# Row scalings and adds in place of diagonal matrix products in a gated S5 + linear-attention kernel

## The chip, the cores and the metric

The kernel runs on one core of one Trainium2 chip. The metric is the device time of one execution in microseconds. Before the change it is 169.73 us, the median of 3 runs (169.57 to 170.41). All work is in bf16 with f32 accumulation; TensorE (PE) multiplies matrices into PSUM, VectorE (DVE), ScalarE (ACT) and GpSimd (POOL) work on 128-partition tiles, and SyncE (SP) issues most DMAs.

## The reference, cut to what matters

The output is `g * a + (1 - g) * b` for 2048 positions of 512 channels, from one input x. The gate g is the sigmoid of one dot product per position.

```python
# a: a diagonal complex state-space layer (512 states)
Lam_bar = exp(dt * Lam);  B_bar = ((Lam_bar - 1) / Lam)[:, None] * Bmat
for t in range(L):  h = Lam_bar * h + B_bar @ x[t]
a = 2 * Re(hseq @ Cmat.T) + x * Dskip
# b: linear attention, 32 heads of 16 channels
phi = concat(softmax(p), softmax(-p))      # of q @ w_phi and of k @ w_phi
b = (phi_q @ (phi_k.T @ v)) / (phi_q @ sum(phi_k)) @ wo
```

## The kernel before, in words

**State-space half.** The 2048 positions are split by residue r = position mod 4, so the scan runs over 512 steps of four positions. x is loaded transposed as `xT`, 16 tiles of 128 positions ordered by residue. For a block j of 128 states (four blocks), `g{j}{dst}{ri}` (`st_g`, L541) multiplies x by B and by the decayed B, LBT = Lam_bar B, for the real or imaginary part ri: `g..0.` is the first phase of two positions (residues 0, 1), `g..1.` the second (residues 2, 3), to which the first, decayed by Lam_bar squared, is added by two products with diagonal matrices (L555, L556). `z{j}` (`st_z`, L581) turns the complex scan into two real scans by rotating with cosine and sine tables (T2c, T2s, made by `i{j}`), and writes the states H3. `h{j}{ri}` (`st_h`, L613) gives the states after the first phase, H1 = M * H3(previous) + U1, by two diagonal products into PSUM (L621, L622) and one DVE add out of PSUM (L625). `c` (`st_c`, L561) makes C2 = C times B's factor by two diagonal products (L575, L576) and a copy out by ACT; `r` and `b` (`st_r` L653, `st_b` L661) make C3 = Lam_bar C2 by one ACT scaling into f32 and one DVE multiply-add. `p` (`st_p`, L531) makes LBT from the loaded B by diagonal products of 256 columns (L535, L536) and an ACT copy. The diagonal matrices `dg` are nine per state block; `D` (`st_D`, L372) builds them on DVE out of `dgs`, the 128 x 1 factors that `M` (`st_M`) computes on POOL.

**Attention half.** `W`, `f`, `w` fold w_phi into the key and query weights. `k`, `v`, `q` (L427 to L446) project a tile of 128 positions by four 512-column products and copy it out of PSUM (`Xq` holds keys, later queries). A feature group is `x` (tree of maxima, subtract), `n` (tree of minima, subtract), `e` (exp on ACT, one 128x1024 instruction a tile), `s` (tree of sums, log, exp, multiply): `feat_max` L465 to `feat_sum` L485. Key groups have two tiles (8 groups), query groups two for the first four tiles (A, B) and four for the rest (X1 to X3). `a` accumulates phi_k.T v and the gate's dot product.

**Tail.** `END` frees pools. For each of 16 output tiles n, in residue order 3, 1, 0, 2: `y{n}` (L692) accumulates the state-space output in a PSUM bank (8 products with H3 or H1, then 4 with K0T or the diagonal Dd), `o{n}` (L713) multiplies phi_q by the key-value matrix (pn), takes the denominator's reciprocal as exp(-ln) on ACT and scales on DVE (L733) into `on`, which a DMA transposes into oT (L739); `t{n}` (L742) adds oT times Wo to the same bank (L746), scales by the gate into `ot` (ACT, or DVE where the token says `:D`) and stores it.

**What sets the order.** `tc.manual_schedule` keeps PE, DVE, ACT and SP in program order, and the program order is the list ORDER: each token is the next step (up to a `yield`) of the generator of that name; `@` gives the PSUM banks (0 to 7) it takes and `:D` puts the step's copy or scaling on DVE in place of ACT. Every engine runs its own instructions strictly in this order and waits by semaphores for the others. DMA transposes are all issued by SP, in its queue, before or in this order. POOL is not in the manual schedule; it runs in the program's order too. The loads of x, B, C and the weights are issued ahead of the list (L221 to L240).

Of the kernel before, what the change touches and what calls it, by code (L numbers as in the profile page):

```python
# [10 lines left out]
ALU = mybir.AluOpType  # L11
AX = mybir.AxisListType
ACT = mybir.ActivationFunctionType
F32 = mybir.dt.float32
# [10 lines left out]
W0@0 V@1 B B V W3@2 U B W0 W2@3 P P P2 P2 W3 U B P2 P2 W2 P2 W1@4 P P4 P3 P4 U W1 f1@5 f2@6 f0@7 f3@1 P4 U P2 v1@0 P3  # L25
v0@2 i1 i0 i1 i0 f1 f2 f3 v1 f0:D i0 k1@3 i0 i0 i2 i1 k1 i1 k0@4 i2 i3 i1 M i2 k0:D i2 k3@5 v0 k2@6 i3 x0 k4@1 n0 k3
x0 n0 v6@7 i2 v5@0 x0 V2@3 n0 i3 i3 k2 x0 n0 k7@4 x0 x1 i3 D k4 n0 v6 L k5@2 n1 k6@5 x1 n1 p32@6 p10@1 x1 e0 p20@7 k6
n1 p02@5 V2 e0 k5:D v3@3 x1 D p30@2 n1 p20 x1 n1 n2 x2 n2 v4@7 s0 p32 x2 v3 s0 x2 s0 p10 e1 v5 n2 k7 p00@6 gw x2 v2@3
p12@1 s0 p30 p22@0 p00 D s0 v7@4 n2 e1 p02 x2 n2 g000@2 s1 s0 n3 s1 x3 n3 x3 v2 s0 g101@6 s1 k8@5 x3 e2 v4 s1 e2 v7 k8
s2 g101 n3 g000 s2 s1 x3 s1 g000 k9@3 a0@74 g001@5 p12 g101 s2 n3 k9 a0 s1 k11@2 s2 x3 n3 s2 s2 e3 n4 x4 n4 k12@1 k11  # L30
a1 x4 k13@6 n4 x4 n4 x4 g001 a1 k10@3 s2 e3 g010@2 x4 k10 n4 a2 s3 n5 g010 g011@3 x5 n5 s3 x5 s3 x5 a2 s3 p22 e4 x5 n5
e4 g011 s4 x5 w3@0 k13 n5 g001 k12 s3 k14@6 s4 w3 n5 s3 s4 g010 v8@5 x6 s3 k14 g011 w1@1 e5 g010 x6 n6 g011 v9@0 s4 s4
a3 v8 e5 w0@6 g100@2 n6 k15@3 v9 s4 x6 z0 z0 n6 z0 k15 x6 g111@5 s5 w1 n6 z0 a3 s4 x6 s5 n6 w0 w2@0 s5 g100 w2 n7 g111
x7 n7 v13@3 g110@1 g100 g111 e6 g110 q1@6 x7 e6 z0 a4 g110 s5 n7 a4 x7 q0@0 v10@2 g111 s6 z0 g110 x7 g200@5 v11@1 n7
s6 x7 n7 s5 z0 v10 s5 g201@2 v13 g211@3 z1 q0 z0 z1 g201 s6 v11 q1 s5 s6 z1 nA z0 e7 e7 z0 xA q2@0 g210@1 g200 s7 s6
g211 nA a5 xA g201 v12@6 z1 nA xA s7 nA s6 q3@2 a5 z1 g210 xA g200 z1 c00@5 s7 z1 q3 xA q2 c00 z1 v12 nA xB z1 nB
v15@2 c13@0 xB s6 g211 eA g310@5 s7 g300@6 g210 eA sA g310 nB v15 g211 s7 g210 sA z1 xB g311@2 z2 z2 nB g301@3 z2
v14@1 s7 g301 nB g300 s7 g311 xB a6 g301 sA z2 g300 g310 sA g311 z2 sA g310 c13 a6 z2 q7@3 sA sA q10@6 z2 g311 xB q8@5
v14 nB c12@0 z2 sA z3 c10@2 eB eB c10 q13@1 a7 q6@2 z3 q13 h01@1 q8 z2 sB c02@5 a7 z3 z3 sA sB c12 z2 q7 z3 Y h01 Y
c01@0 z3 c02 sB q10 c03@3 c11@5 z3 c11 sA q4@6 h00@1 h20@7 c03 sB h21@5 q6 c01 r0 q12@3 h00 z3 sB sB h11@2 G h20 z3  # L40
q12 z3 sB q9@0 h10@1 h10 sB q5@3 h31@7 h30@1 h11 q9 Y q11@0 r1 sB h31 q4 h30 sB h21 q5 END o0@6 Y o0 X1 N1 q11 o1@3 X1
y1@2 N1 q14@7 X1 G K2@0 N1 o0@1 X1 N1 K2 o0 o1 X1 o0 q15@5 N1 o1@4 o0 o1 y1 o0 r1 o0 K3@0 y0@6 q14 o1 q15 K1@7 E1 o1
E1 E1 E1 X2 N2 o1 o3@5 K1 y3@1 N2 X2 o3 o3@3 y2@4 o2@7 o3 N2 y0 b0 K3 o2 y1 S1 N2 o3 S1 y3 X2 S1 r0 o3 y7@0 X2 S1 X2
S1 y2 o2@5 o2 o3 S1 S1 y0 y6@3 y3 N2 S1 o1 t1 G y6 o2 t0 o2 X3 o2 b1 o3 E2 S1 E2 N3 E2 E2 K0@7 t3 G X3 S1 o4@5 t0 o2
y5@6 t1 K0 t3 S2 S2 b0 o4 r2 y2 b1 o5@2 o5 o5@7 o4@1 y5 S1 t3 S1 o5 o4 S2 o5 t2 o5 o5 y4@2 o4 S2 o5 r3 o6@7 S2 y7 o4
o4 o6 S2 b2 y4 S2 o4 o7@5 t2 S2 o6@1 r2 y5 o6 o6 y7 r3 y4 t5 S2 o7 t5 o7@4 b3 o7 X3 X3 b2 b3 y6 t4 o6 y8@6 o6 o7 N3
y9@7 o7 y8 o8@1 N3 o7 S2 o6 y14@5 t4 o9@2 X3 o9 o9@4 N3 t5 y9 N3 o9 o7 o9 o9 E3 t1 S2 o8 t6 o8@2 E3 o8 y8 t7 y14 t6:D
o9 E3 o10@3 o8 E3 t7 o8 o8 o10 S3 S3 y10@4 t0 o10@1 t4 o10 y9 y11@2 o10 t6 S3 o10 S3 o9 t9 o10 y10 S3 S2 t9 o8 o11@0
# [18 lines left out]
def kernel(  # L67
# [96 lines left out]
    nc.scalar.dma_start(out=Wv[:], in_=B_wqkv[:, 2 * D:3 * D].rearrange("(k p) n -> p k n", p=P))  # L164
# [4 lines left out]
    Wk2 = const.tile([P, KT, D], BF16, name="Wk2")  # L169
# [42 lines left out]
    BrT = pAC.tile([P, KT, Pst], BF16, name="BrT")  # L212
    BiT = pAC.tile([P, KT, Pst], BF16, name="BiT")
    LBT = pAC.tile([P, KT, 2, Pst], BF16, name="LBT")
    LBrT, LBiT = LBT[:, :, 0, :], LBT[:, :, 1, :]
# [17 lines left out]
    for ti in range(8, NTI):
        x_load(ti)
    for j in range(KT):
        nc.sync.dma_start_transpose(out=WTq[:, j, :], in_=B_wqkv[:, j * P:(j + 1) * P])
# [581 lines left out]
```

## Time and profile before

| What | Before |
|---|---|
| Median of 3 runs (all) | 169.73 us (170.41, 169.73, 169.57) |
| Span of the profiled execution, first to last instruction | 168.6 us |
| What lies around the span, against the median | 1.1 us |
| PE busy (share), matmuls | 157.2 us (93%), 1062 |
| DVE busy (share), instructions | 145.0 us (86%), 355 |
| ACT busy (share), instructions | 113.2 us (67%), 234 |
| POOL busy | 6.7 us (4%) |
| First projection (pv) / first pn product / last Wo product ends | 9.39 / 99.56 / 165.10 us |
| DMA packets, bytes | 50710, 15.94 MB |

Busy times are sums over the profiled execution. A matmul's listed duration is longer than the interval at which matmuls follow each other: 4 products of 512 columns show as 379 ns each, and a block of four starts every 0.86 us, 0.216 us each. The same holds, by less, for DVE and ACT: an instruction that starts right behind another overlaps its beginning. Below, the interval from start to start in a back-to-back row is called the step, and it is what sums are made of; the steps are read off the start times in the timeline.

### The profile page before, as it was taken

The numbers are of one execution on the slowest core, as the hardware profiler recorded it, in microseconds if no ns is written. First come the engines' busy times: TensorE is split into PE (matmuls) and PEld (weight loads), VectorE is DVE, ScalarE is ACT, GpSimd is POOL, SyncE is SP. The second block draws the span as 40 slices with busy tenths as digits, with TensorE's granted clock in tenths as the row PEclk, the third lists the DMA queues.
The fourth block names the chain that finished last, engine by engine and source line by source line (L and its number), as shares of the span: only waits on it lengthen the run. The fifth ranks groups of instructions, "written<-read, shape, count | busy, mean of one in ns | idle before, by whom it ended". The sixth has DMA issues, their size and how long they took to land.

```text
span 168.6 us, 2978 instructions
## 1 busy us (share of the span) xinstructions
PE 157.2 (93%) x1062; PEld 80.5 (48%) x1062; DVE 145.0 (86%) x355; ACT 113.2 (67%) x234; POOL 6.7 (4%) x23
## 2 busy tenths in 40 slices
PE   0699999999999999999999999999999959999991
PEld 0554466465555544544544444455456424445440
DVE  3796999999999999999999999999999937843540
ACT  3789999989988667374688853974987158404203
POOL 3072010000000000000000000000000000000000
PEclk9999999999999999999999999999999999999999
DMA  4945984546446300000006023111589564669543
GB/s 128 219 92 138 239 136 102 109 95 88 102 93 97 125 2 0 0 4 0 0 4 124 0 53 71 31 35 31 135 179 97 127 171 131 166 159 124 125 125 124
DMA packets 50710, 15.94 MB, mean 95 GB/s; under 512 B 46088, under 2 KB 50696, under 8 KB 50696
## 3 DMA queue, kind: packets, MB, share of 16 engines
q1 hardware_dynamic: 49112, 14.70, 43.1%
q10 hardware_dynamic: 1584, 1.07, 2.2%
q8 instruction: 8, 0.13, 0.4%
q14 instruction: 6, 0.05, 0.1%
HBM read 2.64 MB, written 2.10 MB: 28 GB/s over the span
## 4 chain that ended last, share of the span: by engine, by line
DVE 67%; PE 21%; issue 4%; DMA 4%; ACT 2%; SPq 0%; DVEq 0%; ACTq 0%
DVE smk L460 8%; DVE w L600 5%; PE py L746 5%; DVE EEk L496 5%; DVE mxk L460 5%; DVE mnk L460 5%; PE py L708 4%; DVE EEk L470 4%; DVE EEk L476 4%; DVE on L733 3%; PE py L701 3%; PE py L702 3%; DVE smq L460 3%; DVE H L625 3%; DMA C2r<-in_B_wqkv_dram 2%
## 5 line engine op out<-in xcount | busy, mean ns | idle before, releaser
L425 PEld LDWEIGHTS <-xT 128*128 128x128 bf16 x192 | 18.5, 100 | 20.4 <-issue 2.3
L733 DVE SCALAR_TENSOR_TENSOR on<-pn,RG,rd 128x256 bf16<-128x256 f32 x32 | 14.3, 475 | 10.1 <-ACT rd L134 8.2
L134 ACT ACTIVATE EEk<-EEk 128x1024 bf16<-128x1024 bf16 x20 | 20.9, 1068 | 3.0 <-DVE EEk L476 2.9
L425 PE MATMUL pv<-Wv,xT 128*128 128x512 bf16 x64 | 17.7, 409 | 0.0
L750 ACT ACTIVATE ot<-py,G 128x512 bf16<-128x512 f32 x11 | 7.5, 687 | 13.6 <-PE py L746 8.3
L425 PE MATMUL pq<-Wq,xT 128*128 128x512 bf16 x64 | 16.1, 378 | 0.1
L746 PE MATMUL py<-Wo,oT 128*128 128x512 bf16 x64 | 16.1, 379 | 0.0
L551 PE MATMUL pgq<-xT,LBT 128*128 128x512 bf16 x64 | 15.6, 379 | 0.0
L425 PE MATMUL pk<-Wk,xT 128*128 128x512 bf16 x64 | 15.3, 379 | 0.0
L115 ACT CAST uv<-pgq 128x512 bf16<-128x512 f32 x16 | 9.3, 585 | 6.6 <-PE pgq L551 4.4
L134 ACT ACTIVATE ld<-pn 128x16 f32<-128x16 f32 x32 | 5.4, 186 | 11.0 <-PE pn L724 10.8
L134 ACT ACTIVATE EEq<-EEq 128x1024 bf16<-128x1024 bf16 x12 | 11.9, 1045 | 0.6 <-DVE EEq L476 0.6
L702 PE MATMUL py<-Wv,H 128*128 128x512 bf16 x32 | 12.1, 379 | 0.0
L702 PE MATMUL py<-C2i,H 128*128 128x512 bf16 x32 | 12.1, 379 | 0.0
L701 PE MATMUL py<-Wk,H 128*128 128x512 bf16 x32 | 12.1, 379 | 0.0
L701 PE MATMUL py<-C2r,H 128*128 128x512 bf16 x32 | 12.1, 378 | 0.0
L115 ACT CAST vx<-pv 128x512 bf16<-128x512 f32 x16 | 9.6, 600 | 1.7 <-PE pv L425 1.7
L724 PEld LDWEIGHTS <-phT 128*128 128x128 bf16 x128 | 7.2, 98 | 7.4 <-issue 2.3
L115 ACT CAST Xq<-pq 128x512 bf16<-128x512 f32 x16 | 9.1, 587 | 2.4 <-PE pq L425 2.4
L724 PE MATMUL pn<-KVm,phT 128*128 128x68 bf16 x128 | 8.1, 194 | 2.0 <-ACT ot L750 2.0
L496 DVE TENSOR_TENSOR EEk<-EEk,rck 128x2048 bf16<-128x2048 bf16 x8 | 9.7, 1214 | 0.0
L460 DVE TENSOR_TENSOR smk<-smk 128x512 bf16<-128x512 bf16 (+2 forms) x30 | 9.7, 322 | 0.0
(168 smaller groups left out, 338.0 us busy)
## 6 DMA issues: line engine op xcount, KB each, us to landing
out_dram<-ot SPq DMA_DIRECT2D x16, 128.0 KB, 2.0
C2r<-in_B_wqkv_dram ACTq DMA_DIRECT2D x1, 512.0 KB, 4.0
Wv<-in_B_wqkv_dram ACTq DMA_DIRECT2D x1, 512.0 KB
Bn_r<-in_A_B_re_dram SPq DMA_DIRECT2D x1, 512.0 KB, 4.8
Bn_i<-in_A_B_im_dram SPq DMA_DIRECT2D x1, 512.0 KB
Wo<-in_B_wo_dram SPq DMA_DIRECT2D x1, 512.0 KB
xT<-in_A_x_dram SPq DMA_TRANSPOSE x16, 3.4
oT<-on SPq DMA_TRANSPOSE x16, 2.3
```

The source lines that it names most:

```text
L115: nc.scalar.copy(out=out_ap, in_=in_ap)
L134: ins = nc.scalar.activation(**kw)
L425: MM(out=pt[:], lhsT=xT[:, kt, ti * P:(ti + 1) * P], rhs=W[:, kt, :], start=(kt == 0), stop=(kt == KT - 1))
L460: VT(out=t[:], in0=cur[:, :, :, 0:n, :], in1=cur[:, :, :, n:2 * n, :], op=op)
L496: VT(out=E5, in0=E5, in1=rc[:].to_broadcast([P, L, 2 * NB, Dh, 4]), op=ALU.mult)
L551: MM(out=pgq[:], lhsT=LBT_[:, kt, js], rhs=xT[:, kt, (r1 - 1) * NC:r1 * NC], start=False, stop=(r1 == 1 and kt == KT - 1))
L600: nc.vector.tensor_tensor_scan(out=w[:, ri, :], data0=rb, data1=ut[:, ri, :], initial=0.0, op0=ALU.mult, op1=ALU.add)
L701: MM(out=py[:], lhsT=src[:, j, 0, off:off + P], rhs=cr[:, j, :], start=(j == 0), stop=False)
L702: MM(out=py[:], lhsT=src[:, j, 1, off:off + P], rhs=ci[:, j, :], start=False, stop=False)
L724: MM(out=pn[:, 4 * m:4 * m + 4, :].rearrange("p h e -> p (h e)"), lhsT=ph[:, 4 * hf + m, :], rhs=KVm[:, 4 * hf + m, :], start=(m == 0), st ...
L733: nc.vector.scalar_tensor_tensor(out=on[:, 2 * hf:2 * hf + 2].rearrange("p g h e -> p (g h) e"), in0=pns[hf][:, :, 0:Dh], scalar=RG[:, ti: ...
L746: MM(out=py[:], lhsT=oT[:, g, :], rhs=Wo[:, g, :], start=False, stop=(g == HG - 1))
```

## The change: what it does

- LBT, C2, C3 and H1 are no longer made by products with diagonal matrices (C3: by an f32 scaling and a multiply-add). Each is now two scalings of a real-imaginary pair (128 x 1024, by a 128 x 1 factor, `scaled`, on ACT unless the token says `:D`) and two 512-wide adds or subtracts on DVE; H1 has a 1024-wide add of U1 besides. LBT is then transposed by a DMA from SBUF (`l`, new `st_l`).
- Only the three diagonal matrices of L555/L556 are still built.
- Key groups are now of 2, 2, 4, 4, 2, 2 tiles and the first query group of 4. Their buffers come from one pool.
- DMA transposes are wider: x in 9 DMAs (two of one tile, seven of two), B in 4 from SBUF, Wq in 2, C in 4; and they are issued as steps of the list (`Lx`, `Ln`, `Lb`, `Lq`, `Lc`, `Lo`). The five small parameter loads go from SP to POOL.
- 12 products of a zero tile (`Z`) are issued on PE at the start.
- The gate's factor in the attention output goes into the bias of the exp (L738 after), so that `on` is a two-operand multiply.
- The list ORDER is written anew; all key copies out of PSUM are on ACT, and seven of the `ot` scalings on DVE (five before).

```diff
 ORDER = """
-W0@0 V@1 B B V W3@2 U B W0 W2@3 P P P2 P2 W3 U B P2 P2 W2 P2 W1@4 P P4 P3 P4 U W1 f1@5 f2@6 f0@7 f3@1 P4 U P2 v1@0 P3
...
+Lx Lx Z@0 Z Lx Z Z Z Z Z Z Z Z Z Z V@1 W0@0 V W0 Lx B W2@2 U B W3@3 W3 P W1@4 W1 P B P2 Lx W2 P2 B P2 V2@5 V2 P2 f0@0
+P gw P2 P4 f3@2 U f1@4 P2 f0 f2@3 P4 f3 f1 f2 P3 P4 i0 i2 k0@1 i0 U i0 i0 i0 k1@3 P3 i2 i2 k3@4 Ln k0 Ln k1 Lx Lx Lq U
...
+KGROUPS = ((0, 2), (2, 2), (4, 4), (8, 4), (12, 2), (14, 2))
+XLOADS = ((0, 1), (1, 1), (2, 2), (4, 2), (6, 2), (8, 2), (10, 2), (12, 2), (14, 2))
...
-            nc.sync.dma_start(out=t_[4 * n:4 * n + 4, :], in_=src.rearrange("(j p) -> j p", p=P))
+            nc.gpsimd.dma_start(out=t_[4 * n:4 * n + 4, :], in_=src.rearrange("(j p) -> j p", p=P))
...
+            trans(out=xT[:, :, t0_ * P:(t0_ + n) * P], in_=x_res[t0_ // 4, c0:c0 + n * P])
...
+            trans(out=BT[:, :, :, j * P:(j + 1) * P].rearrange("p r k s -> p (r k) s"), in_=Bn[:, j].rearrange("p r d -> p (r d)"))
...
+    def st_Z():
+        pz = bank([P, D], F32, "pz")
+        while True:
+            MM(out=pz[:], lhsT=warm[:, 0:P], rhs=warm[:], start=True, stop=True)
+            yield
...
+    def scaled(out_ap, in_ap, s_):
+        if sel["eng"] == "act":
+            nc.scalar.mul(out=out_ap, in_=in_ap, mul=s_)
+        else:
+            VS(out=out_ap, in0=in_ap, scalar1=s_, scalar2=None, op0=ALU.mult)
+
+    def st_l(j):
+        lr, li = uv[j][:, 0], uv[j][:, 1]
+        scaled(lr, Bn[:, j], dgs[:, S_LR, j:j + 1])
+        yield
+        scaled(li, Bn[:, j], dgs[:, S_LI, j:j + 1])
+        yield
+        VT(out=lr[:, 0], in0=lr[:, 0], in1=li[:, 1], op=ALU.subtract)
+        yield
+        VT(out=lr[:, 1], in0=lr[:, 1], in1=li[:, 0], op=ALU.add)
+        yield
+        trans(out=LBT[:, :, :, j * P:(j + 1) * P].rearrange("p r k s -> p (r k) s"), in_=lr.rearrange("p r d -> p (r d)"))
+        yield
...
-        MM(out=pc[:], lhsT=dg[:, da, j, :], rhs=CrT[:, j, :], start=True, stop=False)
-        MM(out=pc[:], lhsT=dg[:, db, j, :], rhs=CiT[:, j, :], start=False, stop=True)
-        yield
-        evac(d_[:, j, :], pc[:])
+    def st_c(j):
+        t = (Wo, K0T)[j % 2]
+        a_, b_ = t[:, 0:2, :], t[:, 2:4, :]
+        scaled(a_, CT[:, j], dgs[:, S_BR, j:j + 1])
+        yield
+        scaled(b_, CT[:, j], dgs[:, S_NBI, j:j + 1])
+        yield
+        VT(out=C2[:, 0, j], in0=a_[:, 0], in1=b_[:, 1], op=ALU.add)
+        yield
+        VT(out=C2[:, 1, j], in0=b_[:, 0], in1=a_[:, 1], op=ALU.subtract)
+        yield
...
+    def st_h(j):
+        sw = pools["sw"][1]
         U1 = uv[j][:, 0]
+        prev = H3[:, j, :, ZP - 1:ZP - 1 + NC]
+        mc = sw.tile([P, 2, NC], BF16, name="mc")
+        scaled(mc[:], prev, dgs[:, S_MR, j:j + 1])
+        yield
+        ms = sw.tile([P, 2, NC], BF16, name="ms")
+        scaled(ms[:], prev, dgs[:, S_MI, j:j + 1])
+        yield
+        VT(out=mc[:], in0=mc[:], in1=U1, op=ALU.add)
+        yield
+        VT(out=H1[:, j, 0, :], in0=mc[:, 0, :], in1=ms[:, 1, :], op=ALU.subtract)
+        yield
+        VT(out=H1[:, j, 1, :], in0=mc[:, 1, :], in1=ms[:, 0, :], op=ALU.add)
+        yield
...
-        aexp(out=rd[:], in_=ld[:], func=ACT.Exp, scale=-1.0)
+        aexp(out=rd[:], in_=ld[:], func=ACT.Exp, scale=-1.0, bias=nge[:, ti:ti + 1])
...
-            nc.vector.scalar_tensor_tensor(out=on[:, 2 * hf:2 * hf + 2].rearrange("p g h e -> p (g h) e"),
-                                           in0=pns[hf][:, :, 0:Dh], scalar=RG[:, ti:ti + 1],
-                                           in1=rd[:, hf].unsqueeze(2).to_broadcast([P, 16, Dh]), op0=ALU.mult, op1=ALU.mult)
+            VT(out=on[:, 2 * hf:2 * hf + 2].rearrange("p g h e -> p (g h) e"), in0=pns[hf][:, :, 0:Dh],
+               in1=rd[:, hf].unsqueeze(2).to_broadcast([P, 16, Dh]), op=ALU.mult)
```

`st_r` (C3, into the key and value weights' place) has the form of `st_c`, with the factors of Lam_bar.

More of the change, by code (lines that the diff above doesn't have):

```diff
@@ L233 @@
[L233 to L236, printed above, removed]
-    for kt in range(KT):
-        nc.sync.dma_start_transpose(out=CrT[:, kt, :], in_=A_C_re[:, kt * P:(kt + 1) * P])
-        nc.sync.dma_start_transpose(out=CiT[:, kt, :], in_=A_C_im[:, kt * P:(kt + 1) * P])
-    nc.sync.dma_start(out=Wo[:], in_=B_wo.rearrange("(k p) n -> p k n", p=P))
-    fk_g = tc.tile_pool(name="featK", bufs=3, reuse_waits="tile")
@@ L517, in st_a @@
     def st_a(n):
-        for u in range(2):
-            ti = 2 * n + u
+        first, L = KGROUPS[n]
+        for u in range(L):
+            ti = first + u
             if ti == 0:
```

362 lines of the change are left out of this document (161 added, 201 removed).

## The prediction

> **What bounds the kernel now.** I read the slices of the page first, then busy time by stretch, then the groups by shape, the waits, and SP's timeline. Slices of 4.2 us:
>
> ```profile
> PE   0699999999999999999999999999999959999991
> DVE  3796999999999999999999999999999937843540
> ACT  3789999989988667374688853974987158404203
> ```
>
> PE is full from slice 3 to the last but one; DVE is full to slice 31 and then has room; ACT has room from slice 12 on. By stretch (length, then busy time and instructions of PE, weight loads, DVE, ACT, POOL):
>
> ```profile
> 9.40:16.30 6.90, 6.90 (x27) 2.86 (x26) 5.37 (x12) 6.24 (x13) 4.01 (x11) 1.00 0.45 98
> 16.30:99.50 83.20, 82.98 (x578) 42.43 (x577) 83.17 (x210) 66.43 (x122) 0.63 (x1) 1.00 0.36 69
> 99.50:165.10 65.60, 63.52 (x430) 31.86 (x427) 50.82 (x100) 34.63 (x91) 0.00 (x0) 1.00 0.55 114
> ```
>
> The first phase (to the first pn product, 99.56) is full on PE and on DVE; the tail is full on PE alone. A busy PE need not be at its peak, so I test it with steps: a 512-column product starts 0.216 us after the one before (four in 0.86), one of 256 columns 0.109, of 128 0.056, a pn or kvacc product 0.033, a gate column 0.028. The products from the first projection (9.39) to the first pn sum to 88.3 us; the first eight start 0.42 apart, 1.7 more; 99.4 against 99.56. So PE never stands. The rest sums to 63.3 in a tail of 65.5 (to 165.10). Then come 3.5 us of last scaling and store.
>
> DVE's steps: add of 512 bf16 0.335, 1024 0.60, 2048 1.135, 256 0.20, scan 1.135, f32 multiply-add of 512 0.66, add out of PSUM 0.60, `on` 0.395. From the first feature (16.28) to the first `on` they sum to 89.4, so 105.7; it started at 106.42. So DVE does not stand there either. ACT's steps: exp of 1024 0.95, copy out of PSUM 0.47, scaling of 512 by a tile's column 0.62.
>
> **The change part by part.**
>
> *PE loses:* these groups go.
>
> ```profile
> L535 PE MATMUL pl<-dg,Bn_r 128*128 128x256 bf16 x16 | 3.7, 273 | 0.0
> L536 PE MATMUL pl<-dg,Bn_i 128*128 128x256 bf16 x16 | 3.7, 272 | 0.0
> L622 PE MATMUL ph<-H,dg 128*128 128x512 bf16 x8 | 3.1, 382 | 0.0
> L621 PE MATMUL ph<-H,dg 128*128 128x512 bf16 x8 | 3.0, 379 | 0.1
> L576 PE MATMUL pc<-CiT,dg 128*128 128x512 bf16 x8 | 3.0, 378 | 0.0
> L575 PE MATMUL pc<-CrT,dg 128*128 128x512 bf16 x8 | 3.0, 378 | 0.0
> ```
>
> 32 x 0.109 + 32 x 0.216 = 10.4 us. The built instruction order of the two kernels shows them gone, so that the change does less than it says is no rival. All stood ahead of the first pn. In the new order that place is filled with later work: all 16 q (14 before), the products of all four K0T blocks (7.1, one block before) and 12 py. PE's sum from the first projection to the first pn is 89.3 (88.3), and **its tail is 51.9 (63.3)**.
>
> *ACT gains.* 30 scalings of 1024 (LBT 6, C2, C3 and H1 8 each), 26 of them ahead of the first pn. None of that shape is in the trace. Its row is the C3 scaling of 512 beside the exp of 1024:
>
> ```profile
> L134 ACT ACTIVATE EEk<-EEk 128x1024 bf16<-128x1024 bf16 x20 | 20.9, 1068 | 3.0 <-DVE EEk L476 2.9
> L656 ACT ACTIVATE CrT<-C2r,dgs 128x512 f32<-128x512 bf16 x4 | 2.9, 731 | 0.0
> ```
>
> Not under the exp's step 0.95, not over two of 512, 1.24. The sine of 512 without a tile's column steps 0.52, the cosine with one 0.62; so I take 0.95 + 0.1 = 1.05, 31.5 us. Off go 8 LBT and 8 C2 copies (7.6), 8 small scalings (5.0), two `ot` (1.1); three copies come from DVE (1.4). Net 19; by bounds 16 to 25. From its first weight copy to the first pn's log, ACT's sum is 95.0 (72.9 before, 21.6 idle). ACT was cover; now it is a third full engine.
>
> The Trainium skill, ScalarE: Activation LUTs (What ACT_TABLE_LOAD costs), has ACT at one element a cycle whatever the type and adds about 93 ns for each column operand; the two rows above agree (0.52 to 0.62). Its Rules for kernel authors would put multiplications on VectorE, which it has up to three times faster in bf16; that speaks against these 30.
>
> *DVE is about even.* Off: 8 adds out of PSUM (4.8), 8 f32 multiply-adds (5.3), two of three diagonal builds (1.9), three copies (1.8), 2.7 from wider groups (a 4-tile max tree 1.27, two 2-tile ones 2 x 0.77; the others alike). On: adds for LBT, C2, C3 24 x 0.335 = 8.0, for H1 4 x 0.60 + 8 x 0.335 = 5.1, two `ot` 1.3, a zero tile 0.3, and two scalings of 1024 on DVE. The last are not in the trace: between a 512 scaling in f32 (0.40) and a 1024 add (0.60); I take 0.45, 0.9. Sum -0.9. From first feature to first `on` 89.4 (89.4), after it 42.9 (41.9). `on` with two operands in place of three I leave at 0.395: the nearest two-operand row from PSUM (KVm, 256) ends in 0.40 as well; bounds 0 to -2.2 us in all, in the tail, where DVE has room.
>
> *Start.* The copies of Wk and the identity must be there for W. Five loads move from SP to POOL, ahead of the identity. POOL issues no DMA in the trace: from SP's small loads (0.25 to 0.38 each) to its transposes (1.26) five cost 1.6 to 6.3 us; the identity was ready at 1.82, so 3.4 to 8.1, against the 4.80 at which W began:
>
> ```profile
> 4.80 0.61 PE L276 MATMUL ptw<-ident,C2r 128*128 128x128 bf16 x4 [4.80 <-DMA C2r<-in_B_wqkv_dram]
> ```
>
> I take W at 5.5 (near SP's small loads, since these move 1 KB). The 12 warm products stand before it, 12 x 0.42 from 1.2: 6.2 at worst. From W to the last fold copy took 6.1, now with a fourth copy on ACT 6.6: first key product 12.1. Then 1.9 of sine and cosine on ACT and two copies: first feature at 15.0 (16.28; -0.7 to +2.6 around mine by the POOL bounds).
>
> The cold products:
>
> ```profile
> 9.39 3.52 PE L425 MATMUL pv<-Wv,xT 128*128 128x512 bf16 x8
> 12.75 4.48 PE L425 MATMUL pk<-Wk,xT 128*128 128x512 bf16 x20
> ```
>
> eight in 3.36 us, then 0.216 apart, while the granted clock reads 1.00 throughout; the warm products should take that loss (1.7) off the path. The Trainium skill, TensorE: Matmul & The Clock Gate (Part 1), has half rate until about 3.4 us of sustained work and again after an idle window as long; the spacing bears out the first. If the gap between fold and first key product, some 1.5 us, closed it again, 1.7 us would come back.
>
> *Transposes.* One of 256 KB (phT, 1.23 to 1.30 to issue, 3.0 to land) costs SP what one of 128 KB does (xT, 1.26, 3.4). So x takes 9 issues, not 16, and all of it is in the queue some 15 us sooner; at worst twice the issue, then as now. LBT gets a DMA (1.3 + 3) in place of a copy, and a wait for DVE in SP's queue with the last x tiles behind it, which key tile 14 needs late. I cost it at 0; its cover is the 20 projections (17 us) ahead of the first pgq, without it 4 us once.
>
> **Sum.** The first pn waits for three things. PE: 12.1 + 89.3 = 101.4 (ACT, 5.9 + 95.0 = 100.9, is just ahead). Its phT: the half of the first query group that holds it ends 81.2 us of DVE steps after the first feature, 96.2, and two transposes (issued one behind the other, 2.6, then 3 to land) bring it at 101.8. The second half of the key-value matrix: 86.6 of steps, 101.6. I add 0.8 for engines that wait for each other without slack: **102.6** (99.56). Tail 51.9 + 2.5 (2.2 were lost before): 157.0. Then 3.5: **span 160.5** against 168.6; with the 1.1 between span and median, **161.6**.
>
> **The rivals.**
> 1. *Packed.* First pn at 101.8, tail with 0.5 lost: 101.8 + 52.4 + 3.5 = 157.7, time 158.8. For: before, two engines were full with no gap for 83 us. Against: now it must be three.
> 2. *SP sets the tail.* Its in-order queue holds 12 phT (1.3), 16 oT (1.2), 16 stores (0.5), 43 us of issue; before, first oT 107.35 to the end took 61.3. If the tail keeps that length: first oT 105.2 (first `on` 104.4 and its second half) + 61.3 = 166.5, time 167.6. For: waits of phT and oT on DVE and for each other; against: many waited for PE, which now has less.
> 3. *ACT becomes the bound: slower.* C2 and H1 chains go ACT-DVE-ACT, and each copy from a bank stands in the same queue; PE waits for its banks, DVE for mc and ms. Each us of ACT idle between first weight copy and first pn moves the end. ACT idled 21.6 there; it decides from 9.8 idle on (100.9 + 9.8 = 110.7, and 110.7 + 54.4 + 3.5 = 168.6). With 12: time 171.9. The skill's advice for VectorE, above, is this case.
>
> **How the numbers follow.** Forecast 0.50 (159.3 to 165), rival 1 0.17, rival 2 0.18, rival 3 0.15, of which 0.03 lie within 0.5%, about what a measurement of this kernel can tell from no change. Faster 0.85, same 0.03, slower 0.12. The range, 157.5 to 168.0, reaches to rivals 1 and 2, holds the POOL and ACT bounds, and leaves out rival 3.
>
> **What would show it.** The first pn near 103 and 54 us from there to the last Wo product; ACT over 90% busy from 6 to 103; scalings of 1024 at a step of 1.05; first key product by 12 at 0.216 spacing. Wrong: SP busy without gap behind the first oT (rival 2); PE waiting on ACT copies ahead of the first pn (rival 3); W later than 7.

## The result, and the profile after

The changed kernel takes 171.09 us (median of 20 runs, 169.49 to 171.89) beside 170.1 us for the kernel before, in the same session: a ratio of 1.0055 (95% interval 1.0029 to 1.0081), **slower by half a per cent** where 161.6 us was forecast. The profiled execution has a span of 170.0 us (before 168.6; forecast 160.5).

The slices of the changed kernel, now of 4.25 us:

```profile
PE   7487999999999999999999999999689979988690
DVE  2259899999999999999999999999999957653332
ACT  3079899999999999999999987869994595314110
PEclk9955799999999999999999999999999999999999
```

ACT has become a third full row, as forecast, up to slice 23. PE, full before but for one dent (slice 33), now has dents from slice 29 on: the diagonal products did go, and the time they took is idle. PEclk starts with a hole that the kernel before did not have. By stretch (length, then PE, weight loads, DVE, ACT, POOL busy), from the first pn (106.19) over the first `on` (109.4) and DVE's first long wait (137.7):

```profile
106.19:109.40 3.21, 3.16 (x32) 1.89 (x32) 3.21 (x9) 3.12 (x10) 0.00 (x0) 1.00 0.41 75
109.40:137.70 28.30, 25.88 (x178) 12.84 (x180) 28.29 (x62) 21.83 (x43) 0.00 (x0) 1.00 0.59 118
137.70:150.00 12.30, 11.20 (x75) 5.45 (x75) 6.91 (x15) 6.19 (x19) 0.00 (x0) 1.00 0.63 134
150.00:170.00 20.00, 13.28 (x85) 5.97 (x85) 7.34 (x14) 3.90 (x14) 0.00 (x0) 0.98 0.64 135
```

PE is busy 53.5 of the 63.8 us behind the first pn; in the kernel before it was 63.5 of 69.0. DVE is busy 28.29 of the 28.30 us up to 137.7. Its timeline there shows the first long wait, and for whom:

```profile
136.95 0.74 DVE L759 TENSOR_SCALAR ot<-py,G 128x512 bf16<-128x512 f32 x1
139.73 1.23 DVE L491 TENSOR_TENSOR sm<-EE 128x2048 bf16<-128x2048 bf16 x1 [2.04 <-ACT EE L134]
```

From its first feature instruction (18.70) to 137.70 DVE has no gap of more than 0.34 us: **119.0 us**. In the kernel before it ran as gaplessly from 16.28 to 135.74: **119.5 us**. From there to the end come 32.3 us here and 32.9 us there. The wait itself is not the same one: here DVE waits for the exps of the last query group, in the kernel before its next `on` waits for ACT's reciprocal, and an `ot` scaling ahead of that one on ACT had waited for a store:

```profile
137.95 0.48 DVE L733 SCALAR_TENSOR_TENSOR on<-pn,RG,rd 128x256 bf16<-128x256 f32 x1 [2.21 <-ACT rd L134]
136.28 0.69 ACT L750 ACTIVATE ot<-py,G 128x512 bf16<-128x512 f32 x1 [5.04 <-DMA out_dram<-ot]
```

Where the 9.5 us between forecast span and measured span lie: the first pn came at 106.2 in place of 102.6 (3.6); from there to the end of the last Wo product it took 59.5 in place of 54.4 (5.1); and 4.3 in place of 3.5 from there to the end (0.8).

The start, on PE:

```profile
1.25 4.87 PE L291 MATMUL pz<-warm 128*128 128x512 bf16 x12 [1.25 <-DVE warm L160]
8.64 0.16 PE L296 MATMUL pvt<-ident,vec_n 12*128 12x12 bf16 x1 [2.53 <-DMA vec_n<-in_A_log_dt_dram]
8.73 1.72 PE L283 MATMUL ptw<-ident,C 128*128 128x128 bf16 x16
...
13.87 0.59 PE L455 MATMUL pk<-WKV,xT 128*128 128x512 bf16 x1 [0.41 <-ACT WKV L115]
```

The warm products end at 6.12; then PE stands 2.53 us for a 1 KB vector, loaded from POOL's queue, which V's small transpose needs. W, whose data and identity were there by 5.2, stands behind V in PE's order and begins at 8.73 (forecast 5.5). The sixteen W transposes take 1.72 us. The clock by stretch (the column ahead of the last two):

```profile
6.10:8.60 2.50, 0.01 (x1) 0.00 (x0) 0.52 (x5) 0.00 (x0) 0.00 (x0) 1.00 1.30 209
8.60:12.00 3.40, 2.67 (x23) 2.09 (x24) 1.83 (x14) 2.50 (x7) 0.14 (x1) 0.55 0.97 190
12.00:14.00 2.00, 1.59 (x15) 1.39 (x14) 1.93 (x9) 1.99 (x4) 1.18 (x4) 0.50 1.02 349
```

It was 1.00 through the warm products and the gap, and falls to 0.55 and 0.50 right behind it. The Trainium skill, TensorE: Matmul & The Clock Gate (Part 1), has the clock close after an idle window of about 3.4 us, and calls the window free-running. The trace does not bear out that length: here an idle stretch of 2.5 us was enough. The forecast had named this case and its price (1.7 us), for another gap.

### The profile page after: what moved, and what is told of

Same layout as the page of the kernel before. It is cut to its first block, busy times and chain, and to the rows that moved or that the text cites. A ratio compares the mean times of both kernels' runs of the same rounds, so it can differ in the third digit from the quotient of the medians.

```text
span 170.0 us, 2839 instructions
## 1 busy us (share of the span) xinstructions
PE 153.4 (90%) x991; PEld 75.5 (44%) x1010; DVE 142.4 (84%) x335; ACT 130.4 (77%) x235; POOL 8.9 (5%) x28
## 4 chain that ended last, share of the span: by engine, by line
ACT 43%; PE 19%; DVE 15%; DMA 14%; issue 4%; SPq 2%; POOL 1%; DVEq 1%; POOLq 0%
ACT EE L134 9%; ACT Xq L115 8%; DMA oT<-on 5%; ACT vx L115 5%; DMA vec_n<-in_A_log_dt_dram 3%; ACT uv L115 3%; DVE on L741 3%; ACT uv L395 3%; PE py L709 3%; DVE sm L491 3%; ACT Wo L395 2%; ACT K0T L395 2%; DMA CT<-in_A_C_im_dram 2%; PE py L753 2%; PE py L708 2%
## 5 line engine op out<-in xcount | busy, mean ns | idle before, releaser
L134 ACT ACTIVATE EE<-EE 128x1024 bf16<-128x1024 bf16 x32 | 32.4, 1080 | 1.1 <-DVE EE L508 1.0
L455 PEld LDWEIGHTS <-xT 128*128 128x128 bf16 x192 | 18.9, 100 | 24.2 <-issue 4.6
L741 DVE TENSOR_TENSOR on<-pn,rd 128x256 bf16<-128x256 f32 x32 | 12.2, 416 | 8.3 <-ACT rd L134 4.4
L455 PE MATMUL pk<-WKV,xT 128*128 128x512 bf16 x63 | 17.1, 418 | 1.0 <-ACT WKV L115 0.8
L572 PE MATMUL pgq<-xT,BT 128*128 128x512 bf16 x64 | 16.1, 379 | 0.0
L455 PE MATMUL pv<-WKV,xT 128*128 128x512 bf16 x60 | 15.1, 379 | 0.2
L134 ACT ACTIVATE ld<-pn 128x16 f32<-128x16 f32 x32 | 4.9, 179 | 10.7 <-PE pn L728 10.4
L709 PE MATMUL py<-C,H 128*128 128x512 bf16 x32 | 12.1, 379 | 0.2
L708 PE MATMUL py<-WKV,H 128*128 128x512 bf16 x30 | 11.4, 378 | 0.7 <-DVE on L741 0.4
L491 DVE TENSOR_TENSOR sm<-EE 128x2048 bf16<-128x2048 bf16 (+1 forms) x10 | 10.0, 1002 | 2.2 <-ACT EE L134 2.2
L709 PE MATMUL py<-WKV,H 128*128 128x512 bf16 x30 | 11.4, 379 | 0.1
L708 PE MATMUL py<-C,H 128*128 128x512 bf16 x29 | 11.0, 379 | 0.0
L753 PEld LDWEIGHTS <-oT 128*128 128x128 bf16 x64 | 5.6, 98 | 10.4 <-DMA oT<-on 5.2
L508 DVE TENSOR_TENSOR EE<-mn,Xq 128x2048 bf16<-128x2048 bf16 (+1 forms) x10 | 10.0, 1001 | 0.0
L502 DVE TENSOR_TENSOR EE<-Xq,mx 128x2048 bf16<-128x2048 bf16 (+1 forms) x10 | 10.0, 1001 | 0.0
```

Source lines behind the costliest of these rows:

```text
L134: ins = nc.scalar.activation(**kw)
L455: MM(out=pt[:], lhsT=xT[:, kt, ti * P:(ti + 1) * P], rhs=W[:, kt, :], start=(kt == 0), stop=(kt == KT - 1))
L491: VT(out=dst, in0=cur[:, :, :, 0:n, :], in1=cur[:, :, :, n:2 * n, :], op=op)
L502: VT(out=half(EE, 0), in0=X5, in1=live["mx", p].to_broadcast([P, L, 8, Dh, 4]), op=ALU.subtract)
L572: MM(out=pgq[:], lhsT=BT[:, ri, kt, js], rhs=xT[:, kt, r1 * NC:(r1 + 1) * NC], start=(kt == 0), stop=False)
L708: MM(out=py[:], lhsT=src[:, j, 0, off:off + P], rhs=cw[:, 0, j], start=(j == 0), stop=False)
```

## The experiments

All eighteen in one table. "First feature" is DVE's first max instruction, "`on`" the first scaling of the attention output, "wait" the moment when DVE runs out of work and waits for the last query group's exps (in the kernel before and e13: for ACT's reciprocal; in e6, e10 to e12 and e15 other waits of up to 1.5 us lie ahead of it); spans and moments are of the profiled execution, ratios of the timed runs against the kernel before. Kernels with an unchanged start put the first feature anywhere from 17.8 to 18.9, so that one profile's end is good to about 1 us; the stretches between the columns are steadier.

| Kernel | Ratio to before (95%) | First feature | First `on` (after it) | Wait (after first feature) | Span (after the wait) |
|---|---|---|---|---|---|
| before | 1 | 16.28 | 106.43 (90.1) | 135.74 (119.5) | 168.6 (32.9) |
| after | 1.0055 (1.0029-1.0081) | 18.70 | 109.43 (90.7) | 137.70 (119.0) | 170.0 (32.3) |
| e1 | 0.9911 (0.9882-0.9940) | 15.71 | 106.77 (91.1) | 135.03 (119.3) | 167.0 (32.0) |
| e2 | 0.9989 (0.9959-1.0019) | 16.98 | 107.37 (90.4) | 135.62 (118.6) | 168.0 (32.4) |
| e9 | 0.9929 (0.9896-0.9961) | 15.72 | 106.46 (90.7) | 134.73 (119.0) | 166.4 (31.7) |
| e13 (before) | 0.9924 (0.9881-0.9967) | 15.15 | 105.30 (90.1) | 134.64 (119.5) | 165.9 (31.3) |
| e5 | 0.9993 (0.9959-1.0028) | 18.16 | 108.71 (90.6) | 136.97 (118.8) | 168.2 (31.2) |
| e3 | 1.0043 (1.0016-1.0070) | 18.27 | 108.83 (90.6) | 137.53 (119.3) | 168.3 (30.8) |
| e4 | 1.0026 (0.9999-1.0054) | 17.95 | 108.51 (90.6) | 137.54 (119.6) | 167.7 (30.2) |
| e18 | 0.9946 (0.9915-0.9976) | 17.08 | 107.50 (90.4) | 137.50 (120.4) | 166.8 (29.3) |
| e6 | 1.0100 (1.0066-1.0134) | 18.10 | 109.34 (91.2) | 137.33 (119.2) | 169.9 (32.6) |
| e7 | 1.0734 (1.0662-1.0806) | 18.91 | 119.69 (100.8) | 149.55 (130.6) | 181.4 (31.8) |
| e10 | 1.0188 (1.0146-1.0231) | 18.55 | 110.89 (92.3) | 138.88 (120.3) | 170.7 (31.8) |
| e11 | 0.9989 (0.9958-1.0021) | 15.87 | 107.63 (91.8) | 135.62 (119.8) | 167.5 (31.9) |
| e12 | 1.0018 (0.9988-1.0049) | 17.04 | 108.81 (91.8) | 138.75 (121.7) | 168.0 (29.2) |
| e15 | 0.9872 (0.9822-0.9922) | 16.85 | 106.80 (90.0) | 135.07 (118.2) | 166.5 (31.4) |
| e14 | 1.0322 (1.0243-1.0402) | 17.80 | 108.42 (90.6) | 136.68 (118.9) | 175.1 (38.4) |
| e16 | 1.0372 (1.0321-1.0423) | 18.35 | 108.98 (90.6) | 137.25 (118.9) | 174.7 (37.4) |
| e17 | 1.0331 (1.0260-1.0403) | 15.76 | 106.29 (90.5) | 135.34 (119.6) | 172.9 (37.6) |
| e19 | 1.0079 (1.0051-1.0107) | 15.86 | 106.29 (90.4) | 134.55 (118.7) | 168.4 (33.8) |

### The start: e1, e2, e9

```diff
-            nc.gpsimd.dma_start(out=t_[4 * n:4 * n + 4, :], ...)     # e1, e9
+            nc.sync.dma_start(out=t_[4 * n:4 * n + 4, :], ...)
-... Z V@1 W0@0 V W0 Lx B W2@2 U B W3@3 W3 P W1@4 W1 P B ...          # e2, e9
+... Z W0@0 W0 Lx B W2@2 B W3@3 W3 W1@4 W1 B W2 Lx B f0@0 V@1 V U P P ...
```

> The changed kernel with its five small vector loads back on SP's queue, ahead of the x loads. Theory (the late start is V waiting for its vector, and all three full engines of the first phase are shifted by it): the vectors land by about 4 us, W begins near 6.2 (behind the 12 warm products) in place of 8.73, the first feature comes 2.5 to 4.5 us earlier, the first pn at 102 to 104 in place of 106.2, the span 166 to 168 in place of 170.0. Rival (ACT, filled by the scalings, sets the first phase whatever the start): the first pn stays within 1 us of 106.2 and the span of 170.0.

> The changed kernel with the step list altered at its head alone: the four W steps and one fold stand ahead of V on TensorE, and the loads stay on POOL. Theory: TensorE's strict order, not the loads themselves, costs the time; W begins near 6.2 right behind the warm products, the clock is not closed by the gap of 2.5 us, the first key product starts by 11.5 in place of 13.87 and its products step 0.216 in place of 0.42, the first pn is at 102 to 104, the span 166 to 168. If it is the landing of the vectors itself that counts (sine and cosine tables are needed for the first g steps), the first pn moves by under 1 us.

> Both repairs of the start together: the vector loads on SP as in e1_loads_on_sp and the step list's head as in e2_w_ahead_of_v. e1 brought the first feature to 15.71 and the span to 167.0, e2 to 16.98 and 168.0 with the first key product at 10.59. Theory (the whole of DVE's stretch hangs on the first feature): the first key product at 10.4 to 10.7, the first feature at 14.6 to 15.2, 3.5 to 4 us earlier than in the changed kernel, and the span the same amount shorter, 166 to 166.5. If ACT or TensorE holds the first phase, the span does not follow the first feature.

The profiled ends came out as expected (167.0, 168.0, 166.4), and so did W in e1 and e2 (6.54, 6.69; 5.44 in e9). In the timed runs e2 gains less than e1 (0.9989 beside 0.9911). e9's first feature did not come as expected: 15.72 in place of 14.6 to 15.2. Its first key product was at 9.34, earlier than the expected 10.4 to 10.7, yet the copy of it stands on ACT behind a table load and the sines, and came at 14.47; in the timed runs e9 is no better than e1. PE in e1:

```profile
1.24 5.24 PE L291 MATMUL pz<-warm 128*128 128x512 bf16 x12 [1.24 <-DVE warm L160]
6.41 0.18 PE L296 MATMUL pvt<-ident,vec_n 12*128 12x12 bf16 x1
6.54 1.05 PE L283 MATMUL ptw<-ident,C 128*128 128x128 bf16 x16
...
11.24 0.38 PE L455 MATMUL pk<-WKV,xT 128*128 128x512 bf16 x1 [1.14 <-ACT WKV L115]
```

No gap ahead of V; the W transposes take 1.05 us in place of 1.72 and a key product shows 0.38 in place of 0.59, because the clock is still at 1.00. The first feature moves by 3.0 us and the end by 3.0: what the start loses is lost for good. The changed kernel's own start, against before, cost 2.4 us of first feature, more than the half per cent that it lost; and e1, the changed kernel with one word altered, is 0.9% faster than the kernel before and 1.4% faster than the changed one (0.9911 / 1.0055).

### Does PE set the tail? e5, and e13 on the kernel before

```diff
             MM(out=py[:], lhsT=src[:, j, 0, off:off + P], rhs=..., start=(j == 0), stop=False)
-            MM(out=py[:], lhsT=src[:, j, 1, off:off + P], rhs=..., start=False, stop=False)
```

> The changed kernel, but each y step leaves out its four products with the imaginary part of the state (half of the C products, so the output is not the reference's). TensorE loses 16 x 4 x 0.216 = 13.8 us, nearly all behind the first pn. Theory (SP's queue and the transposes set the tail, so fewer products do not shorten it): the tail from the first pn to the end, 63.8 us, loses under 3 us. Rival (TensorE still sets the tail, as my sum had it): it loses 10 us or more.

> The kernel before, with each y step leaving out its four products with the imaginary part of the state (half of the C products, so the output is not the reference's): 16 x 4 x 0.216 = 13.8 us of TensorE, nearly all behind the first pn. My prediction's view (the tail of the kernel before is full on TensorE alone, so that its length is TensorE's sum): the tail loses 10 us or more, span 155 to 158.5 in place of 168.6. New theory (DVE, which runs without a gap of over 0.15 us from 16.28 to 135.74, and then the chain of the last four tiles, 32.9 us, set the end before too): the span loses under 2.5 us, 166 to 168.5.

In both kernels 13.8 us of products gone from PE shorten the stretch from the first `on` to the end by 1.1 us (60.6 to 59.5; the granted clock reads 0.89 in its last 18 us, 0.98 in the changed kernel's last 20) and 1.6 us (62.2 to 60.6, clock 1.00). e13's span, 165.9, is just under its expected 166 to 168.5, but 1.1 of its 2.7 us are an earlier first feature, which the edit does not touch; the timed runs win 0.8%. For the kernel before, the stretches from the first `on` (length first, PE's busy time second, DVE's fourth):

```profile
106.40:135.70 29.30, 28.58 (x203) 14.85 (x202) 29.20 (x59) 19.29 (x44) 0.00 (x0) 1.00 0.49 96
135.70:150.00 14.30, 12.98 (x85) 6.37 (x85) 7.72 (x15) 8.23 (x21) 0.00 (x0) 1.00 0.59 156
```

and the same stretch of e13:

```profile
105.30:134.60 29.30, 22.25 (x164) 11.01 (x163) 29.20 (x59) 18.66 (x44) 0.00 (x0) 1.00 0.44 99
```

The same 29.30 us, with the same 29.20 of DVE, whether PE has 28.58 or 22.25 us of work in it. PE was full there, and it did not matter. Behind this stretch PE had room in both (28.0 us busy of the last 32.9, and 24.1 of 31.3 in e13). This is the step on which the forecast fell, shown on the very kernel whose profile it was read from.

### Does SP's queue set it? e3, e4, and what adds up, e18

```diff
-... t0 ...  (third step of each t: the store)          # e3, e18
+... t0:A ...                                           # issued by ACT's queue
-        for u in range(L):                              # e4, e18
-            trans(out=dst(u), in_=EE[:, u].rearrange("p m s f -> p (m s f)"))
+        for u in range(0, L, 2):
+            trans(out=dst(u), in_=EE[:, u:u + 2].rearrange("p l m s f -> p (l m s f)"))
```

> The changed kernel with the 16 stores issued from ACT's queue in place of SP's. Theory (SP's in-order queue sets the tail): 16 x 0.53 = 8.5 us of issue leave SP, and no transpose stands behind a store that waits for its scaling, so TensorE's 8 us of idle in the tail shrink to 3 to 5, and the span is 165 to 167 in place of 170.0; the first pn stays at 106. Rival (the chain from DVE's feature to the landed transpose sets the tail, wherever stores are issued): the span stays within 1 us of 170.0.

> The changed kernel with each phT transpose taking two tiles (512 KB in one issue, 8 issues in place of 16). Rival (SP's in-order queue of transposes sets the tail): if one of 512 KB costs SP what one of 256 KB does, 8 x 1.3 = 10 us of issue go and the span falls by 3 to 6 us. New theory (DVE's steps to 137.7, then the chain of the last four tiles): DVE's stretch keeps its 119 us, and only the chain behind it (32.3 us) can shrink or grow, by under 1.5 us; if the issue doubles instead, nothing changes on SP and the landing of the last pair comes up to 1.3 us later.

> The changed kernel with its start repaired (e9, span 166.4), the stores on ACT's queue (e3, tail 1.1 us shorter) and the phT transposes in pairs (e4, tail 1.4 us shorter); nothing left out. e14 showed what a transpose costs that stands ahead of another on SP: four phT and three stores moved ahead of four oT made TensorE wait 4.25 us for one Wo product and the end come 6 us later. Theory (the tail is the ring through SP's in-order queue): what leaves SP shortens it, and the two pieces add: span 163.5 to 164.5, faster than the kernel before by 1.5 to 2.5%. If they do not add: 165 to 165.5.

Rival 2 named SP's issue time. Taking the stores away left the timed ratio where it was (1.0043 beside 1.0055), with 1.1 us off the profiled tail; pairs took 1.4 off. A pair costs SP 1.99 us on the median (1.73 to 3.08) where two singles cost 2.5, so the eight save 3.6 us of issue (20.4 to 16.8), not the 10 of my upper case. Together, in e18, the stretch behind DVE's wait is as short as in any run but e12 (29.3), but DVE's own stretch grows by 1.4 us, because three of DVE's steps for the query groups (`dl`, the difference of two logs, `on`, and the scaling by `rho`, its exponential) now wait for ACT where they had not (0.35 to 0.67 us), and the timed kernel (0.9946) is no better than e9 alone (0.9929). The expected 163.5 to 164.5 was missed by over 2 us. Issue time on SP alone is not the bound.

### DVE, ACT or PE? e6, e7, e10, e11, e12, e15

```diff
-        yield from tree(X5, L, ALU.min, "mn", ("mn", p))     # e6, e10, e11, e12
+        for _ in range(4): yield
-        VT(out=half(live["EE", p], 1), in0=live["mn", p]...
+        VT(out=half(live["EE", p], 1), in0=live["mx", p]...
-        if sel["eng"] == "act": nc.scalar.mul(...)            # e7: all scalings by VS (DVE)
-        scaled(lr, Bn[:, j], ...); scaled(mc[:], prev, ...)   # e10 to e12: LBT's, H1's on DVE (e15: LBT's)
-                VT(out=E5[:, u:u + 2], ..., in1=rc...)        # e15: keys not normalised
```

> The changed kernel without the min trees: the minus half of each feature is shifted by the maximum too, which its normalisation cancels (the result stays the reference's as long as exp of a head's range does not overflow). DVE alone loses work: six 4-tile trees of 1.27 and four 2-tile trees of 0.77, 10.7 us; TensorE, ACT, SP and every order stay as they are. New theory (DVE sets the time: in the changed kernel it runs without a gap from the first feature at 18.70 to 137.7, 119.0 us, as before from 16.28 to 135.74): the end of DVE's full stretch moves by 7 to 10.7 us, until TensorE (13.87 + 1.7 cold + 89.3 + 51.9 + 2.5 + 3.5 = 162.8) is the next bound: span 161 to 164 in place of 170.0. Rival (ACT, 88.5 of 90.7 us busy in the first phase): first pn not before 105, span 168 or more. Rival (transposes on SP): span 168 or more with an early end of DVE's stretch.

> The changed kernel with all 30 scalings of 1024 that ACT does on DVE instead (two are there already and step 0.41). New theory (DVE sets the time): DVE's stretch without gap grows by 30 x 0.41 = 12 us, from 119 to about 131, and the span to 179 to 183. Rival (ACT, filled by 30 x 1.05 = 31.5 us of scalings, sets the first phase): the first pn comes earlier than 106.2 and the span falls by 2 us or more.

> The changed kernel without the min trees (DVE -10.7), and with the 14 scalings of LBT and H1 that ACT did now on DVE (DVE +14 x 0.41 = 5.7, ACT -14 x 1.05 = -14.7). e6 took 10.7 us from DVE alone and moved nothing, because DVE then waited for ACT; e7 took 31 us from ACT alone and DVE ran 12 longer. Theory (first phase: DVE, ACT and TensorE all full, so that only the next one counts): TensorE is left, 13.4 + 1.7 + 89.3 + 0.8 = 105.2 for the first pn, 1 us earlier than in the changed kernel; and the tail from the first on, 59.2 to 60.8 in every version so far, keeps that length: span 167.5 to 169. Rival (ACT and DVE together held the tail as well): the tail falls under 57, span 161 to 165.

> e10 together with the repaired start of e9 (its first key product was at 9.34, its first pn at 103.22, held by DVE from 15.72 on). Theory (three full engines): with DVE and ACT relieved, TensorE is left, 9.34 + 1.7 + 89.3 + 0.8 = 101.1 for the first pn, 2 us earlier than in e9, and 5 earlier than in the changed kernel; the tail from the first on stays at 59 to 60.5: span 163 to 165. If the relief is worth nothing beside the start, it stays at e9's 166.4.

> e11 with the stores on ACT's queue (e3) and the phT transposes in pairs (e4); singly these took 1.1 and 1.4 us off the tail. Theory (the tail is a ring of in-order queues: TensorE waits for landed transposes, ACT's log for TensorE's pn, and the exps behind that log, DVE for the exps, so each piece gives a little): the tail from the first on at 57.5 to 58.5, span 161 to 163.5. If the pieces do not add up: the span of e11 within 1 us.

> e9 (start repaired), without the normalising products of the key features (left out: 8 on DVE of 1.13, 9.1 us; the output is not the reference's) and with the six LBT scalings of ACT on DVE (DVE +2.4, ACT -6.3). So DVE and ACT lose 6.6 and 6.3 us ahead of the first on, TensorE nothing. e6 relieved DVE of 8.4 us of min steps there, but the max steps, now one behind the other, took 3.0 longer and DVE waited for ACT; e10's DVE did 1.6 more than the changed kernel's. Theory (DVE and ACT hold the stretch from the first feature, TensorE comes next): the first on comes 4 to 6.5 us earlier than in e9 (106.46), the end with it, span 160 to 163. If TensorE holds the first phase, the first pn stays at 103 and the span at 165 or more.

e7 is as expected: twelve us more on DVE make the kernel 11.6 us longer from first feature to wait, though ACT does 31 us less. **So ACT alone (rival 3) is not the bound, and DVE has no slack.** The page's chain of work that ended last runs 67% on DVE in the kernel before and 43% on ACT in the changed one, so its shares do not name the one engine to relieve. And e6, where DVE does less, moved nothing, so that "DVE sets the time" is only half of it. In e6 by stretch (length, PE, weight loads, DVE, ACT):

```profile
18.10:60.00 41.90, 41.90 (x287) 20.91 (x286) 37.50 (x74) 41.57 (x67) 1.10 (x5) 0.98 0.40 73
60.00:100.00 40.00, 39.76 (x269) 19.52 (x268) 37.15 (x76) 39.94 (x62) 0.00 (x0) 1.00 0.22 41
```

DVE has room now; PE and ACT have none. The waits say so too (who waited for whom, us in all, times, longest):

```profile
DVE sm L491 <- ACT EE L134: 2.8, 3, 1.5
DVE mx L491 <- ACT Xq L115: 2.5, 5, 0.9
```

e15 relieves both DVE (6.6) and ACT (6.3):

```profile
16.90:60.00 43.10, 42.65 (x287) 21.19 (x292) 41.96 (x107) 37.91 (x65) 2.43 (x8) 1.00 0.54 86
60.00:103.50 43.50, 43.03 (x283) 21.19 (x286) 38.99 (x84) 41.45 (x64) 0.00 (x0) 1.00 0.19 40
```

and PE is the one that stays full throughout: from first feature to first `on` it is busy 88.98 of 89.95 us, DVE 84.30, ACT 82.62. The first pn stays at 103.55 (103.22 in e9), as the alternative in its expectation said. e10 shows the same: PE 91.80 of 92.34 us, DVE 88.94, ACT 75.57. So in the first phase three engines are full side by side (PE 89.89, DVE 90.23, ACT 88.57 of 90.73 us in the changed kernel), and a gain on one or two is worth next to nothing; e15's timed runs are the fastest, by 0.6% beside e9, with intervals that overlap. No run takes work from all three.

My expectations for e6 and e15 were wrong by this omission. e10 and e11 failed at a second point. Their first pn came 0.2 and 1.0 us behind what was expected (105.4 and 102.1), but the first `on` stands 5.5 us behind it in place of 3.2, with four of the H1 scalings now between the two on DVE. DVE was not busier for it (88.94 us in e10, 90.23 in the changed kernel); it stands for 3 us on the way, 2.5 of them waiting for ACT. In e6 the 24 max steps behind the first of each tree ahead of the first `on` take, from start to next start, 7.43 us in place of 4.43; 2.0 of the 3.0 are waits for ACT. e12 adds e3 and e4 to e11 and gains nothing in the timed runs.

### The order of the tail: e14, e16, e17, e19

```diff
-... t5 S3 o8@3 y6 ... S3 o8 y13 S3 S3 ... S3 (thirteen S3 spread up to o13)
+... t5 S3 S3 S3 S3 S3 o8@3 ... o8 S3 S3 S3 S3 y13 ... o9 S3 S3 ... o10 S3 S3   # e14; e19: the first nine only
```

> The changed kernel, with the last query group's 13 steps (its sums, log, second scaling and four transposes) moved up in the step list, ahead of the on steps of tiles 8 to 11; no instruction is added or taken away. In every version so far DVE's stretch from the first feature to its wait for that group's exps took 119 us (118.6 to 121.7), and the end came 29 to 33 us after it. Theory (that second stretch is the chain of the last group: sums, transposes, pn, on, transposes, Wo products): its four phT transposes are issued by 149 in place of 154.6, and the end comes 27 to 30 us behind the wait in place of 32.3, span 164.5 to 168. If TensorE's leftover work sets the second stretch: no gain, span within 1 us of 170.

> e14 with half of the C products left out as in e5 (the output is not the reference's). TensorE's work in the tail falls by some 12 us. Theory: with the last group early, TensorE's leftover work is what is next in the second stretch, so that now fewer products count: the end comes 23 to 27 us behind DVE's wait, span 160 to 165. If the landing of the transposes is all that counts: the same as e14 within 1 us.

> The changed kernel with the start repaired (e9), the last group early (e14) and the phT transposes in pairs (e4), nothing left out. Theory, by adding: e9 is at 166.4, e4 took 1.4 to 2.1 off the tail, e14 is to take 2 to 5: span 160 to 164, faster than both kernels by 2.5% or more. If e14 gives nothing: 165.

> e9 with the last group's nine steps on DVE and ACT (sums, log, second scaling) moved up as in e14, but its four phT transposes left in their old places on SP's queue. Theory (e14's loss came from SP: oT transposes behind phT transposes, and TensorE waiting for them): without that, no loss: tail from the first on within 1 us of e9's 59.9, though the last multiplication by rho ends 2 to 3 us earlier. If DVE's order alone made the loss in e14 (on steps delayed behind the sums), the tail is again 64 us or more.

Not one instruction more, and e14 is 6 us slower from first `on` to end (66.7 in place of 60.6); e17, with the start repaired, likewise. SP's queue in e14:

```profile
145.04 5.37 SPq L544 DMA_TRANSPOSE phT<-EE  x4
150.47 1.55 SPq L760 DMA_DIRECT2D out_dram<-ot  x3
152.07 5.12 SPq L745 DMA_TRANSPOSE oT<-on  x4
```

The last group's four phT did go out by 150.4 (154.6 in the changed kernel), as planned; but the oT transposes of finished tiles now stand behind them, and PE, whose order has their Wo products next, stands:

```profile
155.81 1.89 PE L752 MATMUL py<-Wo,oT 128*128 128x512 bf16 x4 [4.25 <-DMA oT<-on]
```

e19, which leaves SP's order alone, loses 2.2 us beside e9 (62.1 in place of 59.9; expected: under 1), where e14 loses 6.1 beside the changed kernel: about two thirds of e14's loss is SP's order. That the rest comes from DVE's `on` behind the sums is argued, not shown. e16 shows that even then PE's products count for 1 us. So the waits read as a ring of in-order queues: PE's pn waits for a landed phT, ACT's log for pn, the exps behind that log, DVE's `on` for ACT, SP's oT for `on`, PE's Wo product for oT. The changed kernel's waits in the tail go round it:

```profile
ACT ld L134 <- PE pn L728: 10.4, 9, 2.9
PEld L753 <- DMA oT<-on: 5.0, 5, 1.8
DVE on L741 <- ACT rd L134: 4.4, 4, 1.3
PEld L728 <- DMA phT<-EE: 3.5, 4, 1.0
PE py L753 <- DMA oT<-on: 3.2, 3, 1.3
```

**Still open:** which list would make the tail shorter. Which link of the ring would have to give is not shown. Removing work from any one member took at most 1.6 us off it, my one rearrangement made it longer, and none better than 59.2 us was found. That a new list could turn PE's idle time into an earlier end is neither shown nor excluded.

## Why the prediction was wrong, point by point

- **"The tail is full on PE alone", hence "Tail 51.9 + 2.5": wrong, the larger part of the miss** (59.5 in place of 54.4). PE's busy time behind the first pn did fall by 10 us (63.5 to 53.5), but the tail's length was not PE's: e13 takes 13.8 us of products out of the kernel before and wins 1.6. The same profile held the stretch that I did not sum: DVE without a gap until 135.74, 119.5 us behind the first feature, and 32.9 us from there to the end. I read "DVE is full to slice 31 and then has room" as room in the tail; slices 25 to 31 are the tail's first half. With these two stretches on my own first feature, 15.0 + 119.5 + 32.9 = 167.4: a gain of 1.2 us, not 8. What sets the 32.9 us is open; that it is not PE's sum is shown.
- **The start: wrong by 3.7 us at the first feature** (18.70 against 15.0), of which 3.6 arrive at the first pn. I costed the identity's delay (ready at 5.18, inside 3.4 to 8.1) and the copy of Wk, but not the landing of the moved vectors, which V needs ahead of W in PE's order (landed 5.92 us after issue). My mark "W later than 7" caught it. The clock then closed, as the sentence on the 1.7 us had it.
- **First phase: right in its working.** The sum let the latest of three paths decide, DVE's steps with phT behind them: 86.8 us behind the first feature, and 0.8 on top, 87.6. The first pn follows the first feature by 87.5 us here, 87.8 in e1, 87.1 in e2 and 87.5 in e9. PE's path (89.3 + 0.8 behind the first key product) did not decide: the first pn comes 92.3 us behind that product here, some 2 of them cold clock, and 93.9 in e9, whose key products begin 4.5 us earlier. ACT's scalings of 1024 step 1.04 (three in 3.22 us), 1.05 forecast; ACT is busy 79.95 us of the 80 from 20 to 100. DVE's two step 0.40 (0.45 forecast).

```profile
L395 ACT ACTIVATE CT<-C,dgs 128x1024 bf16<-128x1024 bf16 x8 | 9.3, 1184 | 0.0
L397 DVE TENSOR_SCALAR uv<-Bn,dgs 128x1024 bf16<-128x1024 bf16 x2 | 0.9, 476 | 0.0
```

- **`on` with two operands**: 416 ns in place of 475, a step of 0.335; so the lower bound (some 2 us of DVE less) was right and not the value taken, and it is not seen in the end.
- **Rival 2 (the tail keeps its length)** was nearest in what the tail did: 59.5 us from the first oT, 61.3 before. Its cause, SP's issue time, was wrong (e3, e4); its order does matter (e14). **Rival 3** had the sign, and its 171.9 was the nearest time, but by luck: it needs over 9.8 us of ACT idle ahead of the first pn's log, and ACT is idle 2.9 of the 99.2 us from its first weight copy on. ACT is full but gives DVE its data in time, and e7, with 31 us less on ACT, is slower. **Rival 1** asked for a faster tail, like the forecast.
- **The sign.** The net gain on PE, 10 us, is real (PE idle 10.3 us of the last 63.8, 5.6 of 69.0 before); it could not become time, since DVE's sum stayed (119.0 for 119.5) and the ring behind it too (32.3 for 32.9). What is left is the start's 2.4 us, less 1.0 from these two.

## What to carry to other kernels

When several engines are full under one fixed order, sum every one of them from its first to its last step before crediting a saving: here two engines had next to no gap over the same 119 us, and taking work from one was worth 1.6 us of 13.8. The cheap test is the reverse of the change: leave out products in the old kernel (its output is then not the reference's) and see whether its end moves, before rebuilding it around that saving. And follow a moved load to the first instruction that waits for it, with everything that stands behind that instruction: a 1 KB vector cost more here than all the products brought.

## What the runs showed of the hardware that was not expected

- Five loads of 1 KB from POOL's queue took 0.52 us each to issue (the first 0.77), 0.26 to 0.38 from SP's (e1), and landed 4.7 to 6.0 us after issue; the transposes of x were under way beside them.
- The granted clock closed right behind an idle stretch of 2.5 us (1.00 to 0.55), and read 0.50 from 12 to 18 us, with key products 0.42 apart; in e1 it stayed at 1.00 to 12 us, fell to 0.78 and 0.50 behind PE's waits at 10 to 12, and recovered by 17.
- A DVE step that reads what the step just ahead of it wrote starts 0.03 us behind that one's listed end (e6: 18.11 and 0.43 long, the next at 18.57). A step of another tree starts 0.08 us ahead of it (changed kernel: 18.70 and 0.42 long, the next at 19.04).
- A phT transpose of 512 KB holds SP for 1.99 us on the median (e4, 1.73 to 3.08), one of 256 KB for 1.26 and an oT transpose of 128 KB for 1.22 (changed kernel): cheaper by the byte, but not free.
